# Layer 0 of a two-layer MLP in blocks of 512 tokens, weights converted in place, and attention banks shared

## The chip, the cores and the metric

One core of a Trainium2 chip runs the kernel. The metric is device time in microseconds of one execution, the median of several. The engines are TensorE (PE in the profile, its weight loads PEld), VectorE (DVE), ScalarE (ACT), GpSimd (POOL) and SyncE (SP), whose queue issues all DMAs here.

## What is computed

Sliding-window attention, then two MLP layers, all in float32. The weights come as float64 bits and are turned into float32 on the chip.

```python
# q, k, v: (4, 8, 576, 64); window 128; ALiBi slope per head
scores = where(0 <= i - j < 128, q @ k.T / 8 - slope * (i - j), -1e9)
x = softmax(scores) @ v            # -> (2304 tokens, 512)
h = maximum(x @ w_in, 0)           # layer 0, w_in (512, 2048)
x = (h * h) @ w_out                #          w_out (2048, 512)
h = x @ w2_in                      # layer 1
out = (h * cos(h)) @ w2_out
```

## The kernel before

**Tiling.** There are 18 blocks of 128 tokens for the attention; an attention step is one such block with two heads, so there are 72 steps. The 2048 hidden features of a layer are 16 `f` tiles of 128. A float32 operand of an MLP product is split into a high and a low part, and a product is three matmuls (hi·hi, lo·hi, hi·lo; lines 465 to 467 for `h`, 528 to 530 for `y`), each with weights of 128x128 and a moving operand of 256 or 512 tokens.

**Units.** The MLP work is a list of units, `ORDER`. In layer 0 a unit is 256 tokens and two `f` tiles, in layer 1 it is 512 tokens and one `f` tile; only layer 1's last block has 256 tokens. Each of these units writes one PSUM bank of `h` (2 x 256 or 512 float32) and adds to the banks of `y`. The first two and the last two blocks of layer 0 take turns (`CUTS`, `END_CUTS`): a block runs some `f` tiles, its partial `y` waits in SBUF (`YS`, `y_out`), and the other block follows.

**The main loop** (line 655) goes through the units. For unit i it emits: the softmax of an attention step, `h_mms(i + 1)`, the ReLU and square of unit i + 1 (`relu_part`, `square_part`), the transposes of the step, `y_mms(i)` and the step's product with V (`values`). `need` says how many attention steps must be out after each unit. Before the loop the first 16 steps run by themselves. A scheduler then sets the order on each engine, and each engine executes its list in that order.

**Weights.** `w_job` turns half an `f` tile (512 float64 per partition) into float32: a DMA into one of three `raw_w` buffers; `f64_top` (ACT) writes the upper half-words into `upper`, one tile for all; `f64_rest` (DVE) joins them with the lower bits into one of three `cv` buffers; `w_hi` (ACT) and `w_lo` (DVE) split that into `wh` and `wl`. Weights of layer 1 take the places of those of layer 0.

**PSUM** has eight banks: four for `y` and `h` of layer 0 (two each), two for the scores `s`, one for the transposes `t`, one for the attention output `o`. In the first 16 steps every other scores tile lies in an `h` bank (line 321).

Of the kernel before, what the change touches and what calls it, by code (L numbers as in the profile page):

```python
# [22 lines left out]
P = 128  # L23
NJ = NT // P
T = 256
# [19 lines left out]
ORDER = [  # L45
    (0, n, fs)
    for n0, n1, cuts in TURNS
    for a, b in zip(cuts, cuts[1:])
    for n in (n0, n1)
    if n is not None  # L50
    for fs in PAIRS[a:b]
]
ORDER += [(1, b, (f,)) for b in range(NB // 2) for f in range(NF)]
ORDER += [(1, NB // 2, fs) for fs in PAIRS]
NG1 = NB * NU
# [7 lines left out]
A_OPEN, W_OPEN, START_W, W1_FROM = 8, 1, 2, 64  # L63
# The first units leave more of their squares to the scalar engine.
ACT_UNITS = 20


class Job:
    """One piece of operand preparation: a load, then stages on ACT and DVE."""

    def __init__(self, key, load, stages, gates=None, source=None):
        self.key, self.load, self.stages = key, load, stages
        self.gates, self.source = gates or {}, source
        self.raw, self.at = None, 0
# [3 lines left out]
def attention_mlp_mlp(ctx: ExitStack, tc: tile.TileContext, kq, k0, q0, v, w1, w2, bias, ident, out):  # L78
    """Sliding-window ALiBi attention, relu^2 MLP, h*cos(h) MLP, in float32.

    Activations lie with features on the partitions and tokens on the free
    dimension.  A float32 operand of the MLP products is split exactly into
    hi + lo (float32r parts); a product is hi*hi + hi*lo + lo*hi.
    """
# [4 lines left out]
    cst = ctx.enter_context(tc.tile_pool(name="cst", bufs=1))  # L89
    wp = ctx.enter_context(tc.tile_pool(name="wp", bufs=1))  # L90
    rp = ctx.enter_context(tc.tile_pool(name="rp", bufs=4))
    cv = ctx.enter_context(tc.tile_pool(name="cv", bufs=3))
    xp = ctx.enter_context(tc.tile_pool(name="xp", bufs=1))
    gp = ctx.enter_context(tc.tile_pool(name="gp", bufs=2))
    yp = ctx.enter_context(tc.tile_pool(name="yp", bufs=2))
    dp = ctx.enter_context(tc.tile_pool(name="dp", bufs=1, space=DRAM))
    ps_y = ctx.enter_context(tc.tile_pool(name="ps_y", bufs=1, space=PSUM))
    ps_h = ctx.enter_context(tc.tile_pool(name="ps_h", bufs=2, space=PSUM))

    halfpi = cst.tile([P, 1], F32, name="halfpi")  # L100
    upper = cst.tile([P, 512], F32, name="upper")

    y1 = [dp.tile([P, KT * T], F32, name=f"y1_{n}") for n in range(NB)]

    WH, WL, A2, Y, YS = {}, {}, {}, {}, {}
# [7 lines left out]
    RAWS = {"a": 3, "w": 3}  # L113
# [19 lines left out]
    def advance(job):  # L133
        job.stages[job.at](job)
        if job.at == 1:
# [46 lines left out]
    def f64_rest(job):  # L182
        """The 19 lower bits of the significand, from the next 32 bits of the float64."""
        job.t = cv.tile([P, 512], F32, tag="cv", name="cv_" + "_".join(map(str, job.key)))
# [4 lines left out]
            upper.bitcast(I32),  # L189
# [14 lines left out]
    def w_job(layer, f, half):  # L204
        """Weights of layer 1 take their places when layer 0 has done with them."""
# [4 lines left out]
            [  # L210
                f64_top,
# [3 lines left out]
            {0: lambda: layer == 0 or now["y"] >= W1_FROM, 2: lambda: now["y"] >= max(last, default=-1)},  # L215
        )

    # x of two blocks of 256 tokens, hi and lo; layer 1 has a second such pair of tiles
    XS = [[xp.tile([P, 2, KT, T], F32R, name=f"x{part}_0") for part in "hl"]]

    def x_view(layer, n, part):
        pair = XS[0] if layer == 0 else XS[(n // 2 + 1) % 2]
        return pair[part][:, n % 2]

    def x_ready(layer, n):
        """Whether the units that read what x takes the place of have been emitted."""
        if layer == 0:
            old = [(0, n - 2)]
        else:
            old = [(1, n // 2 - 2)] if n >= 4 else [(0, NB - 1), (0, NB - 2)] if n >= 2 else []  # L230
        return now["h"] >= max((i for i, unit in enumerate(ORDER) if unit[:2] in old), default=-1)

    def x2_job(n, half):
        ks = slice(2 * half, 2 * half + 2)

        def hi(job):
            act.copy(x_view(1, n, 0)[:, ks], job.raw.rearrange("p (a t) -> p a t", a=2))

        def lo(job):
            r = job.raw.rearrange("p (a t) -> p a t", a=2)  # L240
            dve.tensor_tensor(x_view(1, n, 1)[:, ks], r, x_view(1, n, 0)[:, ks].bitcast(F32), ALU.subtract)

        return Job(
            ("x", n, half),
            lambda raw: sp.dma_start(raw, y1[n][:, half * 512 : half * 512 + 512]),
            [hi, lo],
            {0: lambda: len(XS) > 1 and x_ready(1, n)},
            ("y", n),
        )
# [63 lines left out]
    def scores(a):  # L313
        """Scores of one block of queries and two heads, and their exponentials."""
# [447 lines left out]
```

## Time and profile before

| | |
|---|---|
| time, median of 3 runs (lowest to highest) | 954.16 us (953.32 to 954.29) |
| profiled execution: span from first to last instruction | 950.9 us |
| median less that span | 3.3 us |
| PE busy / ACT busy / DVE busy | 932.8 / 528.0 / 604.9 us |

The profile gives one execution, and for it the span alone; what lies around the span is taken as 3.3 us. A matmul's busy time in the profile runs past the start of the next one, so what a matmul costs in a row of matmuls is read from the distance between starts, not from its busy time.

### The profile page before, as it was taken

What the parts mean: (1) busy time and instruction counts of PE and PEld (TensorE: products, weight loads), DVE (VectorE), ACT (ScalarE), POOL (GpSimd) and SP (SyncE); (2) the same over time, 40 slices, a digit from 0 to 9 for tenths busy, and PEclk for the clock granted to TensorE, in tenths of its full rate; (3) what the DMA queues carried; (4) which work ended last, traced back from release to release, by engine and by line L of the source; (5) the groups of instructions that cost most, each with busy time, mean ns of one, the idle gap of its engine ahead of it and who ended that gap; (6) DMA issues with size and microseconds to landing.
All of it is one profiled execution on the core that took longest, in us unless ns stands there. A gap on an engine that the chain in (4) does not pass through costs nothing.

```text
span 950.9 us, 16566 instructions
## 1 busy us (share of the span) xinstructions
PE 932.8 (98%) x6528; PEld 851.7 (90%) x6528; DVE 604.9 (64%) x1409; ACT 528.0 (56%) x1144; POOL 10.0 (1%) x37
## 2 busy tenths in 40 slices
PE   6899999999999999999999999999999999999998
PEld 6699989999999999999999988888888888888898
DVE  5998756555565666556648698566557566655564
ACT  5998766544444555445547586454445445444443
POOL 2000000000000000000000000000000000000000
PEclk9999999999999999999999999999999999999999
DMA  8576632112111121111117561011001100100010
GB/s 240 181 243 227 217 115 90 57 45 77 46 57 46 55 68 38 64 56 46 45 46 239 184 199 44 1 44 45 1 1 39 39 1 1 45 1 1 1 45 23
DMA packets 33965, 71.63 MB, mean 75 GB/s; under 512 B 3424, under 2 KB 10976, under 8 KB 33888
## 3 DMA queue, kind: packets, MB, share of 16 engines
q1 hardware_dynamic: 33888, 70.58, 23.0%
q8 instruction: 51, 0.84, 0.4%
q14 instruction: 26, 0.21, 0.1%
HBM read 61.13 MB, written 9.44 MB: 74 GB/s over the span
## 4 chain that ended last, share of the span: by engine, by line
PE 85%; DMA 5%; ACT 4%; DVE 4%; issue 1%; SPq 1%; ACTq 0%; DVEq 0%
PE y L528 13%; PE y L530 13%; PE y L529 13%; PE h L467 13%; PE h L466 12%; PE h L465 12%; DMA raw_w<-w_in 3%; PE o L423 3%; PE s L339 3%; PE t L406 3%; ACT upper L180 2%; DMA raw_a<-kq_in 1%; DVE cv_w L185 1%; ACT wh L198 1%; ACT p L381 1%
## 5 line engine op out<-in xcount | busy, mean ns | idle before, releaser
L467 PE MATMUL h<-xh,wl 128*128 128x256 f32 (+1 forms) x896 | 281.5, 314 | 0.0
L465 PE MATMUL h<-xh,wh 128*128 128x256 f32 (+1 forms) x896 | 280.7, 314 | 0.3 <-ACT wh L198 0.3
L466 PE MATMUL h<-xl,wh 128*128 128x256 f32 (+1 forms) x896 | 280.6, 313 | 0.0
L467 PEld LDWEIGHTS h<-xh,wl 128*128 128x128 f32 x896 | 170.9, 191 | 11.2 <-issue 1.2
L465 PEld LDWEIGHTS h<-xh,wh 128*128 128x128 f32 x896 | 170.7, 191 | 10.5 <-ACT wh L198 0.5
L466 PEld LDWEIGHTS h<-xl,wh 128*128 128x128 f32 x896 | 170.8, 191 | 9.9
L528 PE MATMUL y<-rh,wh 128*128 128x256 f32 x576 | 169.9, 295 | 1.4 <-ACT rh L479 0.9
L529 PE MATMUL y<-rl,wh 128*128 128x256 f32 x576 | 163.2, 283 | 1.8 <-DVE rl L483 1.8
L530 PE MATMUL y<-rh,wl 128*128 128x256 f32 x576 | 162.8, 283 | 0.0
L528 PE MATMUL y<-gh,wh 128*128 128x512 f32 (+1 forms) x320 | 117.8, 368 | 0.0
L529 PE MATMUL y<-gl,wh 128*128 128x512 f32 (+1 forms) x320 | 117.7, 368 | 0.0
L530 PE MATMUL y<-gh,wl 128*128 128x512 f32 (+1 forms) x320 | 117.7, 368 | 0.0
L528 PEld LDWEIGHTS y<-rh,wh 128*128 128x128 f32 x576 | 109.7, 191 | 7.4 <-issue 4.8
L529 PEld LDWEIGHTS y<-rl,wh 128*128 128x128 f32 x576 | 110.1, 191 | 2.9 <-DVE rl L483 2.6
L530 PEld LDWEIGHTS y<-rh,wl 128*128 128x128 f32 x576 | 110.0, 191 | 0.3 <-issue 0.3
L494 ACT ACTIVATE r<-r 128x512 f32<-128x512 f32 x72 | 45.5, 632 | 114.7 <-DVE r L493 114.6
L371 DVE CUSTOM_DVE_ANT_0 s<-s,bias_sb 128x256 f32<-128x256 f32 (+4 forms) x160 | 62.3, 392 | 55.3 <-PE s L339 37.5
L507 DVE TENSOR_TENSOR gl<-g,gh 128x512 fp32r<-128x512 f32 x72 | 49.8, 691 | 73.1 <-ACT gh L506 73.0
L381 ACT ACTIVATE p<-s,st 128x256 f32<-128x256 f32 (+4 forms) x160 | 70.5, 442 | 44.4 <-DVE st L371 42.2
L491 DVE SCALAR_TENSOR_TENSOR r<-kk,h 128x512 f32<-128x512 int32 x72 | 49.4, 686 | 63.5 <-ACT kk L490 63.5
L490 ACT ACTIVATE kk<-h 128x512 int32<-128x512 f32 x72 | 43.0, 597 | 69.8 <-PE h L467 69.6
L528 PEld LDWEIGHTS y<-gh,wh 128*128 128x128 f32 x320 | 60.3, 189 | 10.0
(63 smaller groups left out, 1312.8 us busy)
## 6 DMA issues: line engine op xcount, KB each, us to landing
raw_w<-w_in SPq DMA_DIRECT2D x64, 511.8 KB, 4.7
raw_a<-kq_in SPq DMA_DIRECT2D x56, 256.0 KB, 2.9
v<-v_in SPq DMA_DIRECT2D x18, 256.0 KB, 2.9
y<-ysb SPq DMA_DIRECT2D x18, 256.0 KB, 2.5
raw_a<-y SPq DMA_DIRECT2D x18, 256.0 KB, 2.8
out<-ysb SPq DMA_DIRECT2D x16, 256.0 KB, 2.9
k<-k_in SPq DMA_DIRECT2D x4, 256.0 KB, 5.5
q<-q_in SPq DMA_DIRECT2D x8, 128.0 KB, 5.5
```

What stands on the lines that cost most here:

```text
L371: dve.tensor_tensor_reduce(out=sbank[p0:p1, e, c0:c1], in0=sbank[p0:p1, e, c0:c1], in1=bias_sb[p0:p1, h, b0 + c0 : b0 + c1], scale=-0.125, ...
L381: act.activation(pt[p0:p1, e, c0:c1], sbank[p0:p1, e, c0:c1], AF.Exp, bias=st[p0:p1, e : e + 1], scale=-1.0, accum_out=st[p0:p1, 2 + e : 3 ...
L465: te.matmul(o, wh[:, cs], xh, start=(c == 0 and kt == 0), stop=False, skip_group_check=True)
L466: te.matmul(o, wh[:, cs], xl, start=False, stop=False, skip_group_check=True)
L467: te.matmul(o, wl[:, cs], xh, start=False, stop=(kt == KT - 1), skip_group_check=True)
L490: act.activation(kk, hb, AF.Copy, scale=INV2PI)
L491: dve.scalar_tensor_tensor(r, kk, -C1, hb, ALU.mult, ALU.add)
L494: act.activation(r, r, AF.Abs)
L507: dve.tensor_tensor(rl, g, rh.bitcast(F32), ALU.subtract)
L528: te.matmul(o, wh, gh, start=(first and m % per == 0), stop=False, skip_group_check=True)
L529: te.matmul(o, wh, gl, start=False, stop=False, skip_group_check=True)
L530: te.matmul(o, wl, gh, start=False, stop=last, skip_group_check=True)
```

## The change

Layer 0 goes over to units of 512 tokens and one `f` tile, like layer 1. Its order is: blocks 0, 1 and 2 of 512 tokens, one after the other; then block 3 (512 tokens) and block 4 (256 tokens) in turns, two units of block 3 and one of block 4 (with two `f` tiles) at a time. There are 72 units in layer 0 as before. All of a block's `f` tiles add up in its own `y` banks, so the partial sums in SBUF are gone. A list `MARKS` says how many attention steps are out by which unit.

A weight's `cv` buffer (two, not three) is set to zero by GpSimd, then `f64_top` writes into it and `f64_rest` joins in place; `upper` is gone. While the attention runs there are four `y` banks, one `h` bank, two banks that scores and transposes share, and one for `o`; the scores of the first 16 steps lie in the `y` banks. A finished `y` bank is copied into the buffers of the ReLU results (`a`, two of them) while the attention runs, and into those and two more afterwards. The cosine part of layer 1 works in place. The first 10 units, not 20, leave their squares to ACT.

```diff
-CUTS = (0, 1, 3, 5, 8)
-END_CUTS = (0, 4, 8)
-PAIRS = [(2 * u, 2 * u + 1) for u in range(NU)]
-TURNS = [(0, 1, CUTS)] + [(n, None, (0, NU)) for n in range(2, NB - 2)] + [(NB - 2, NB - 1, END_CUTS)]
+NBK = NB // 2
+ORDER = [(0, b, (f,)) for b in range(NBK - 1) for f in range(NF)]
+JOINT = len(ORDER)
+for u in range(NU):
+    ORDER += [(0, NBK - 1, (2 * u,)), (0, NBK - 1, (2 * u + 1,)), (0, NBK, (2 * u, 2 * u + 1))]
...
-ACT_UNITS = 20
+ACT_UNITS = 10
...
+    def f64_zero(job):
+        job.t = cv.tile([P, 512], F32, tag="cv", name="cv_" + "_".join(map(str, job.key)))
+        pool.memset(job.t, 0.0)
+
     def f64_top(job):
-        top = upper.bitcast(F16).rearrange("p (n two) -> p n two", two=2)
+        top = job.t.bitcast(F16).rearrange("p (n two) -> p n two", two=2)
...
-        if a < START and a % 2:
-            sbank = ps_h.tile([P, 2, 256], F32, tag="h", name=f"s_{a}")
+        if a < START:
+            sbank = ps_y.tile([P, 2, 256], F32, tag=f"y{a % 4}", name=f"s_{a}")
...
-        tb = ps_t.tile([P, 2, 2, P], F32, tag="t", name=f"t_{s}")
+        tb = ps_s.tile([P, 2, 2, P], F32, tag="s", name=f"t_{s}")
...
+    def h_slot(i):
+        if i >= NG1:
+            return ((ps_h, "h"), (ps_h2, "h"), (ps_y2, "z0"), (ps_y2, "z1"))[(i - NG1) % 4]
+        return (ps_h2 if ps_h2 is not None and i % 2 else ps_h), "h"
...
-        # partial sums of a block wait in SBUF for the rest of its f range
-        if (layer, n) in YS:
-            ysb = YS.pop((layer, n))
-            for b in range(2):
-                dve.tensor_tensor(ysb[:, b], Y[0][b], ysb[:, b], ALU.add)
...
+    def y_out(layer, b):
+        for k, yb in enumerate(Y.pop(b)):
+            if gp2 is not None and k % 2:
+                ysb = gp2.tile([P, 2, T], F32, tag="ysb", name=f"ysb_{layer}_{b}_{k}")
+            else:
+                ysb = gp.tile([P, 2, T], F32, tag="a", name=f"ysb_{layer}_{b}_{k}")
+            (dve.tensor_copy if k % 2 else act.copy)(ysb, yb)
+            if layer == 0:
+                sp.dma_start(y1[b][k], ysb.rearrange("p a t -> p (a t)"))
...
+    MARKS = [(-1, START), (14, 32), (29, 50), (30, 52), (45, 66), (48, STEPS)]
```

**What moves on TensorE, where the MLP begins.** In a tile's name the last number is a running one: before, `h_658` is the first unit's `h` (256 tokens), `o_551` is the output of attention block 3 and `t_570` a transpose. This is TensorE's list before, in the midst of the first unit:

```order
L466 MATMUL h_658<-xl_96,wh_1_654 128x256
L423 MATMUL o_551<-p_459,v_278 64x128 x2
L423 MATMUL o_551<-p_459,v_392 64x128 x2
L467 MATMUL h_658<-xh_95,wl_1_655 128x256
L406 MATMUL t_570<-id_sb,p_459 128x128 x4
L465 MATMUL h_658<-xh_95,wh_1_654 128x256
```

And now, with the waits; `h_652` is the first unit's `h` (512 tokens), `o_554` the output of attention block 3, `s_674` the scores of the 18th step:

```order
L419 MATMUL o_554<-p_530,v_281 64x128 [waits Activation_49]
L419 MATMUL o_554<-p_530,v_281 64x128
L419 MATMUL o_554<-p_530,v_395 64x128 x2
L335 MATMUL s_674<-KS,qh_1_513 128x256 [waits PE_49]
L335 MATMUL s_674<-KS,qh_1_513 128x256
L335 MATMUL s_674<-KS,ql_1_514 128x256 x2
L463 MATMUL h_652<-xh_100,wh_0_272 128x512 [waits Activation_49]
L464 MATMUL h_652<-xl_101,wh_0_272 128x512 [waits DVE_49]
L465 MATMUL h_652<-xh_100,wl_0_273 128x512
```

The first unit no longer stands among the products of the first 16 steps but behind all of them; it reads x of all four attention blocks.

**What moves on ScalarE, where one block of layer 0 ends and the next begins.** Before, in the middle of the attention, `ysb_3` is the result of block 3 (256 tokens), `a_` a ReLU result and `rh_` the high part of its square:

```order
L471 ACTIVATE a_3605<-h_3580 128x512 [waits PE_49]
L408 COPY p_3481<-t_3607 128x512 [waits PE_49]
L481 ACTIVATE rh_3613<-a_3605 128x512 [waits Activation_49]
L554 COPY ysb_3_3655<-y_0_3008 128x512 [waits PE_49]
L282 CAST qh_2_3576<-raw_a_3359 128x256 [waits PE_49]
```

And now at the end of the first block of 512 tokens, where `ysb_0_0` and `ysb_0_2` are copies of `y` banks 0 and 2:

```order
L539 COPY ysb_0_0_2057<-y_0_747 128x512
L377 ACTIVATE p_2074,st_2075<-s_2069,st_2075 128x256 [waits DVE_49] x2
L404 COPY p_1997<-t_2103 128x512 [waits PE_49]
L539 COPY ysb_0_2_2063<-y_2_749 128x512 [waits DMAHW1_49,Activation_49]
L277 CAST KS<-raw_a_2009 128x256 [waits DMAHW2_49]
L278 CAST qh_1_2011<-raw_a_1904 128x256 [waits PE_49]
L469 ACTIVATE a_2101<-h_2088 128x512 [waits DMAHW4_49,Activation_49]
```

The second copy and the next ReLU (`a_2101`) now wait for DMAs, those that empty their buffers.

**What is new on GpSimd.** Before, its list holds no weight at all. Now it holds 64 zeroings, here those of `f` tiles 5 and 6, between the zeroings of softmax tiles `p_`:

```order
L168 MEMSET cv_w_5_1_1055 128x512 [waits DVE_49,Activation_49]
L362 MEMSET p_862 64x2x64 [waits PE_49,Pool_49]
L363 MEMSET p_862 64x2x128
L360 MEMSET p_947 128x2x64 [waits PE_49,Activation_49,Pool_49]
L168 MEMSET cv_w_6_0_1100 128x512 [waits DVE_49]
```

A zeroing waits for DVE's last read of the buffer (`w_lo` of the half tile two before), and those of tile 6 stand behind softmax tiles that wait for TensorE.

## Rows read from the trace of the kernel before

**Rows 1.** The page, parts 1 and 2: busy time; TensorE's granted clock.

```profile
PE 932.8 (98%) x6528; PEld 851.7 (90%) x6528; DVE 604.9 (64%) x1409; ACT 528.0 (56%) x1144; POOL 10.0 (1%) x37
...
PEclk9999999999999999999999999999999999999999
```

**Rows 2.** The page, part 4: the chain that ended last, by engine.

```profile
PE 85%; DMA 5%; ACT 4%; DVE 4%; issue 1%; SPq 1%; ACTq 0%; DVEq 0%
```

**Rows 3.** Groups of TensorE's instructions by line and shape.

```profile
L465 PE MATMUL h<-xh,wh 128*128 128x256 f32 x640 | 181.1, 283 | 0.3 <-ACT wh L198 0.3
L528 PE MATMUL y<-rh,wh 128*128 128x256 f32 x576 | 169.9, 295 | 1.4 <-ACT rh L479 0.9 <-ACT ysb L554 0.5
...
L465 PE MATMUL h<-xh,wh 128*128 128x512 f32 x256 | 99.6, 389 | 0.0
```

**Rows 4.** Timeline of TensorE, layer 0 in its middle: start us, us, what.

```profile
300.33 0.28 PE L465 MATMUL h<-xh,wh 128*128 128x256 f32 x1
...
303.21 0.60 PE L406 MATMUL t<-id_sb,p 128*128 128x128 f32 x4
...
314.88 0.28 PE L465 MATMUL h<-xh,wh 128*128 128x256 f32 x1
```

**Rows 5.** The same in layer 1, units of 512 tokens.

```profile
651.13 0.39 PE L528 MATMUL y<-gh,wh 128*128 128x512 f32 x1
...
656.57 0.39 PE L528 MATMUL y<-gh,wh 128*128 128x512 f32 x1
```

**Rows 6.** TensorE by windows: window, us, busy (x instructions), clock, DMA share, GB/s.

```profile
0.00:50.00 50.00, 39.66 (x325) 1.00 0.70 210
50.00:200.00 150.00, 145.92 (x1229) 1.00 0.46 149
200.00:450.00 250.00, 250.00 (x2191) 1.00 0.18 56
```

**Rows 7.** The same windows, instructions on tile h alone.

```profile
0.00:50.00 50.00, 3.87 (x24) 1.00 0.70 210
50.00:200.00 150.00, 65.93 (x504) 1.00 0.46 149
200.00:450.00 250.00, 106.53 (x840) 1.00 0.18 56
```

**Rows 8.** The same windows, instructions on tile y alone.

```profile
0.00:50.00 50.00, 1.33 (x9) 1.00 0.70 210
50.00:200.00 150.00, 68.18 (x498) 1.00 0.46 149
200.00:450.00 250.00, 111.25 (x823) 1.00 0.18 56
```

**Rows 9.** Timeline of TensorE, its first matmul of the MLP.

```profile
37.24 0.36 PE L465 MATMUL h<-xh,wh 128*128 128x256 f32 x1
```

**Rows 10.** Timeline of ScalarE, x of the fourth attention block.

```profile
49.66 0.59 ACT L437 CAST xh<-o 128x512 fp32r<-128x512 f32 x1
```

**Rows 11.** All engines by windows: PE, PEld, DVE, ACT, POOL busy, then as rows 6.

```profile
50.00:100.00 50.00, 48.09 (x390) 46.88 (x389) 42.11 (x84) 43.54 (x88) 0.00 (x0) 1.00 0.72 239
...
200.00:250.00 50.00, 50.00 (x441) 48.78 (x440) 29.22 (x87) 24.58 (x66) 0.00 (x0) 1.00 0.20 65
```

**Rows 12.** Window 50 to 100 us, instructions on tile h, then on tile y alone.

```profile
50.00:100.00 50.00, 26.52 (x204) 1.00 0.72 239
...
50.00:100.00 50.00, 24.99 (x186) 1.00 0.72 239
```

**Rows 13.** The page, part 6: DMA issues, KB each, us to landing.

```profile
y<-ysb SPq DMA_DIRECT2D x18, 256.0 KB, 2.5
```

**Rows 14.** Groups on GpSimd: busy us, mean ns.

```profile
L617 POOL MEMSET upper<- 128x512 f32 x1 | 0.5, 517 | 0.0
```

**Rows 15.** Waits: us in total, times, longest us.

```profile
ACT p L381 <- DVE st L371: 42.2, 60, 5.3
...
ACT upper L180 <- DMA raw_w<-w_in: 12.2, 10, 2.3
```

More of the change, by code (lines that the diff above doesn't have):

```diff
@@ L34, with __init__ @@
 C2 = 2.0 * math.pi - C1
-CUTS = (0, 1, 3, 5, 8)
-END_CUTS = (0, 4, 8)
-PAIRS = [(2 * u, 2 * u + 1) for u in range(NU)]
-TURNS = [(0, 1, CUTS)] + [(n, None, (0, NU)) for n in range(2, NB - 2)] + [(NB - 2, NB - 1, END_CUTS)]
[L45 to L55, printed above, removed]
+NBK = NB // 2
[3 more added lines that the diff above has]
+    ORDER += [(0, NBK - 1, (2 * u,)), (0, NBK - 1, (2 * u + 1,)), (0, NBK, (2 * u, 2 * u + 1))]
+NG1 = len(ORDER)
+ORDER += [(1, b, (f,)) for b in range(NBK) for f in range(NF)]
+ORDER += [(1, NBK, (2 * u, 2 * u + 1)) for u in range(NU)]
+INDEX = {unit: i for i, unit in enumerate(ORDER)}
 START, LOOK, PLAIN = 16, 2, 4
-A_OPEN, W_OPEN, START_W, W1_FROM = 8, 1, 2, 64
-ACT_UNITS = 20
+A_OPEN, W_OPEN, START_W, W1_FROM = 8, 1, 2, JOINT - 2
+ACT_UNITS = 10
 class Job:
-    def __init__(self, key, load, stages, gates=None, source=None):
-        self.key, self.load, self.stages = key, load, stages
+    def __init__(self, key, load, stages, gates=None, source=None, frees=1):
+        self.key, self.load, self.stages, self.frees = key, load, stages, frees
         self.gates, self.source = gates or {}, source
@@ L188, in f64_rest @@
             13,
-            upper.bitcast(I32),
+            job.t.bitcast(I32),
             ALU.logical_shift_right,
@@ L210, in w_job @@
             [
+                f64_zero,
                 f64_top,
@@ L214, in w_job, with x_slot, x_ready, x2_job @@
             ],
-            {0: lambda: layer == 0 or now["y"] >= W1_FROM, 2: lambda: now["y"] >= max(last, default=-1)},
-        )
[L219 to L230, printed above, removed]
+            {0: lambda: layer == 0 or now["y"] >= W1_FROM, 3: lambda: now["y"] >= max(last, default=-1)},
+            frees=2,
+        )
+    XS = [[xp.tile([P, 2, KT, T], F32R, name=f"x{part}_{i}") for part in "hl"] for i in range(2)]
+    def x_slot(layer, b):
+        return (0, 1, 0, 1, 0)[b] if layer == 0 else (2, 0, 1, 2, 0)[b]
+    def x_ready(layer, b):
+        users = [(0, a) for a in range(NBK + 1)] + [(1, a) for a in range(NBK + 1)]
+        old = [u for u in users[: users.index((layer, b))] if x_slot(*u) == x_slot(layer, b)]
         return now["h"] >= max((i for i, unit in enumerate(ORDER) if unit[:2] in old), default=-1)
-    def x2_job(n, half):
-        ks = slice(2 * half, 2 * half + 2)
+    def x2_job(b, m):
+        def view(part):
+            x = XS[x_slot(1, b)][part]
+            return x[:, :, m, :] if b < NBK else x[:, 0, 2 * m : 2 * m + 2, :]
         def hi(job):
-            act.copy(x_view(1, n, 0)[:, ks], job.raw.rearrange("p (a t) -> p a t", a=2))
+            act.copy(view(0), job.raw.rearrange("p (a t) -> p a t", a=2))
         def lo(job):
             r = job.raw.rearrange("p (a t) -> p a t", a=2)
-            dve.tensor_tensor(x_view(1, n, 1)[:, ks], r, x_view(1, n, 0)[:, ks].bitcast(F32), ALU.subtract)
+            dve.tensor_tensor(view(1), r, view(0).bitcast(F32), ALU.subtract)
         return Job(
-            ("x", n, half),
-            lambda raw: sp.dma_start(raw, y1[n][:, half * 512 : half * 512 + 512]),
+            ("x", b, m),
+            lambda raw: sp.dma_start(raw, y1[b][m]),
             [hi, lo],
-            {0: lambda: len(XS) > 1 and x_ready(1, n)},
-            ("y", n),
+            {0: lambda: len(XS) > 2 and x_ready(1, b)},
+            ("y", b),
         )
@@ L441, in attention_mlp_mlp @@
     Hb, Aa, R2 = {}, {}, {}
-    ypools = [ps_y]
-    hpools = [ps_h]
+    ps_h2 = None
+    def h_slot(i):
+        if i >= NG1:
+            return ((ps_h, "h"), (ps_h2, "h"), (ps_y2, "z0"), (ps_y2, "z1"))[(i - NG1) % 4]
+        return (ps_h2 if ps_h2 is not None and i % 2 else ps_h), "h"
     def h_mms(i):
-        layer, n, fs = ORDER[i]
+        layer, b, fs = ORDER[i]
         if layer == 1:
-            run_until(("x", min(2 * n + 1, NB - 1), 1))
+            for m in range(KT if b < NBK else 2):
+                run_until(("x", b, m))
         for f in fs:
@@ L451, in h_mms @@
         now["h"] = i
-        hb = hpools[i % len(hpools)].tile([P, 2, T], F32, tag="h", name=f"h_{i}")
+        hpool, tag = h_slot(i)
+        hb = hpool.tile([P, 2, T], F32, tag=tag, name=f"h_{i}")
         Hb[i] = hb
@@ L520, in y_mms @@
             cols = slice(512 + m * P, 512 + m * P + P)
-            o = Y[0][m // per]
+            o = Y[b][m // per]
             if per == 2:
@@ new lines, in y_mms @@
+                y_out(layer, b)
+    def y_out(layer, b):
[7 more added lines that the diff above has]
+                sp.dma_start(y1[b][k], ysb.rearrange("p a t -> p (a t)"))
+            else:
+                dst = out[2 * b : 2 * b + 2][:, :, k * T : k * T + T]
+                sp.dma_start(dst.rearrange("n p t -> p n t"), ysb)
+        if layer == 0:
+            finished.add(("y", b))
@@ L572, in y_tail @@
             else:
-                act.copy(ysb[:, m], src)
-            sp.dma_start(out[NB - 1][:, m * T : m * T + T], ysb[:, m])
-    LA = 1
-    need = [0] * (NG1 + 1)
-    for i in range(NG1 - 1, -2, -1):
-        ahead = i + LA + 1
-        req = 8 * (ORDER[ahead][1] + 1) if 0 <= ahead < NG1 else 0
-        rate = 1 if 2 * NU <= i + 1 < NG1 - 2 * NU else 2
-        need[i] = min(STEPS, max(req, (need[i + 1] if i + 1 < NG1 else 0) - rate))
-    start_steps = max(need[-1], START)
-    need = [max(x, start_steps) for x in need]
+                act.copy(ysb, src)
@@ L588, in attention_mlp_mlp, with need @@
+            sp.dma_start(out[NB - 1][:, m * T : m * T + T], ysb)
+    MARKS = [(-1, START), (14, 32), (29, 50), (30, 52), (45, 66), (48, STEPS)]
+    def need(i):
+        for (i0, s0), (i1, s1) in zip(MARKS, MARKS[1:]):
+            if i <= i1:
+                return s0 + (s1 - s0) * (i - i0) // (i1 - i0)
+        return STEPS
+    start_steps = START
+    LA = 1
     pieces = [(f, half) for f in range(NF) for half in range(2)]
@@ L590, in attention_mlp_mlp @@
         queues["a"] += [kq_job(j, hp) for hp in range(4)]
-    queues["a"] += [x2_job(n, half) for n in range(NB) for half in range(2)]
+    queues["a"] += [x2_job(b, m) for b in range(NBK + 1) for m in range(KT if b < NBK else 2)]
     queues["w"] += [w_job(layer, *p) for layer in range(2) for p in pieces]
@@ L616, in attention_mlp_mlp @@
             pool.memset(Q0[j][0:64, :, 1, :], 0.0)
-        pool.memset(upper, 0.0)
         dve.memset(halfpi, math.pi / 2)
```

95 lines of the change are left out of this document (32 added, 63 removed).

## The prediction

> **What bounds the kernel now.** I read the page first: TensorE is busy for 932.8 of 950.9 us, at the full 2.4 GHz (a granted clock of nine tenths or more in every slice) [rows 1], and the chain that ended last lies on it for 85% [rows 2]. Such a busy share alone proves little here, since a matmul's busy time (283 ns with 256 tokens, 389 ns with 512 [rows 3]) overlaps that of the next. So I went on to the distances between starts. In layer 0 the 24 matmuls of `h` start at 300.33 and the next instruction at 303.21 us: 2.88 us, or 120.0 ns each [rows 4]. In layer 1 it is 24 matmuls in 651.13 to 656.57 us: 5.44 us, or 226.7 ns each [rows 5]. Neither stretch has a hole, so TensorE itself is the limit there, and a matmul's price is 120.0 ns for 256 tokens and 226.7 ns for 512. Doubling the tokens adds 106.7 ns, so 13.3 ns of either price come with the instruction and not with its tokens.
>
> The price of an attention step follows from the same stretch: from 300.33 to 314.88 us [rows 4] there are two units (96 matmuls, 11.52 us) and two steps, so a step takes (14.55 - 11.52) / 2 = 1.51 us of TensorE.
>
> With these prices the windows show where TensorE loses time. A step has 16 matmuls. From 200 to 450 us it starts 2191, of which 840 are for `h` and 823 for `y` [rows 6 to 8]: 1663 x 0.120 = 199.6 us, and 528 / 16 = 33 steps make 49.8 us; together 249.4 of 250 us. Nothing is lost. From 50 to 200 us it is 1002 x 0.120 = 120.2 us and 227 / 16 = 14.2 steps, 21.4 us: 141.7 of 150, so 8.3 us are lost. There the first weights are made: between 50 and 100 us ACT is busy for 43.54 and DVE for 42.11 of 50 us [rows 11]. The first 50 us are the attention's start; only 24 + 9 matmuls of the MLP lie in them [rows 7, 8].
>
> **The larger blocks.** Layer 0 has 9 blocks x 16 `f` tiles x 24 = 3456 matmuls of 256 tokens (`y` shows 576 on each of three lines [rows 3]). Now 4 blocks of 512 tokens take 4 x 16 x 24 = 1536 matmuls of 512, and 384 of 256 stay. So 3072 matmuls become 1536, and each pair saves 2 x 120.0 - 226.7 = 13.3 ns: 1536 x 13.3 = **20.5 us less**. This holds only while TensorE is the limit, as it is from 200 us on. Rounding of the starts (0.01 us over 24 matmuls) moves the price by less than 1 ns, the term by 1 us.
>
> The Trainium skill ("TensorE: Matmul & The Clock Gate", section Back-to-back issue gap) gives N / 2.4 + 2.5 ns for a warm matmul, so 109.2 and 215.8 ns: a pair would save 2.5 ns, and the whole term would be 3.8 us. The rows of this case show 120.0 and 226.7 ns with a weight load for every matmul, and the measurement decides.
>
> **The first unit starts later.** Before, its matmuls fill holes of the attention's start, from 37.24 us on [rows 9]. Now they stand behind all 16 steps and wait for x of the fourth attention block, whose cast begins at 49.66 us and takes 0.59 [rows 10]. The 33 matmuls that lay before 50 us [rows 7, 8] thus move behind it, 33 x 0.120 = 4.0 us, with about 1 us for the cast and the scores of a later step that also lay there: **5 us more**. ACT, which paces this stretch, loses the first unit's ReLU and square there and gains weights of later tiles instead; I count these as equal. Bounds: 3 us (the start gets as much shorter as ACT has less) and 6.
>
> **The first block with attention beside it.** While weights are made, units of block 0 now run with one step each; before, nearly no step ran until its end. The TensorE time of these steps is only moved. ACT's load is what counts: from 50 to 100 us it is 43.54 us for 204 + 186 = 390 matmuls of the MLP [rows 11, 12], 390 / 48 = 8.1 units, so 5.36 a unit; from 200 to 250 us it is 24.58 us for 441 matmuls [rows 11], 441 / 64 = 6.9 units with a step each, 3.6 for both; I put ReLU and square, two instructions of about 0.6, at 1.2, which leaves 2.4 for a step. So a unit with weights and step needs about 7.8 us of ACT, against 24 x 0.2267 + 1.51 = 6.95 us of TensorE. The busy times on ACT overlap too, so 7.8 is an upper bound, and I take it that TensorE stays just ahead. Weights are needed more slowly than before (one tile in 6.95 us, not 5.76), so ACT's waits for their DMAs (12.2 us in all [rows 15]) shrink, and the four evictions in turns with their sums fall away. I take **2 us less** of the 8.3; bounds: all 8.3 less, and 16 x (7.8 - 6.95) = 13.6 us more, if ACT sets the pace.
>
> Zeroing is 64 x 0.517 us [rows 14] on an engine that is busy for 10.0 us now [rows 1]; in steady state it lies between the last read of a buffer and the next half tile. With two `cv` buffers it can be late only in this block; its cost is in the bounds above.
>
> **Three hand-overs between blocks.** At the end of blocks 0, 1 and 2 the four copies of `y` go through two buffers, so the third waits for the landing of the first (2.5 us [rows 13]), and the next ReLU for that of the third. The chain is two copies (0.59 each by the cast of that size [rows 10]) and two landings, 6.2 us; beside it TensorE has the next unit's `h`, two steps' work and a `y`, some 7 us. It is late by little, and behind the waiting ReLU on ACT stand only the next square and exponentials. I take 1 us each, **3 us more**; bounds 0 and 3 x 6.2 = 19, where nothing hides it.
>
> **At nothing.** From the second block on a unit has about 1.2 steps, so 7.3 us of TensorE against 1.2 + 1.2 x 2.4 = 4.1 us of ACT. Scores and transposes in two banks: the next scores come one unit later, after the exponentials; uncovered it would be a wait for them on TensorE in each step. Turns at the end: layer 1's weights get 24 units, as long as the first weights had and without attention. Layer 1 keeps its units and its four `h` banks, so its 5.44 us a unit stay.
>
> **The sum.** -20.5 + 5 - 2 + 3 = -14.5 us. Against the profiled execution that is a span of 950.9 - 14.5 = 936.4; the median of the runs lies 3.3 us above the span, so the time is 939.7 us.
>
> **The rivals.**
> *The start and the hand-overs cost nothing much, and the first block's waits go.* -20.5 + 3 - 6 + 0 = -23.5: 930.7 us. For it: half of the 8.3 us may belong to the turns. Against: the new order puts the first unit behind the last step.
> *ACT sets the pace of the first block.* Then the third term is +13.6: -20.5 + 5 + 13.6 + 3 = 1.1, 955.3 us, and half of it gives 948. For it: 43.54 of 50 us before, and steps come on top; ACT executes its list in order, and one exponential alone waited up to 5.3 us for DVE [rows 15]. Against: ACT's true load is less than its busy sum.
> *One `h` bank is too few.* While the attention runs, `h` of unit i + 1 cannot start before the ReLU of unit i has read the bank; between them TensorE has only `y` of unit i - 1 and a step, 2.72 + 1.51 = 4.2 us. Whenever ACT comes to the ReLU later than that, TensorE stands. Averaged over 48 units, 0.3 us each eats the 14.5; at 0.5 us it is 24 us, 964 us. For it: long waits in ACT's list, as above. Against: outside the first block ACT is free for over 40% of the time (4.1 of 7.3 us).
> *The larger instruction saves nothing here.* If a matmul of 512 tokens in layer 0 took as long as two of 256, say because the attention between them spoils it, the sum would be 0 + 5 - 2 + 3 = +6: 960.2 us. Against it: [rows 4, 5], and layer 1 runs the same code.
> By the formula of the Trainium skill quoted above it would be nearly so, -3.8 + 5 - 2 + 3 = +2.2, 956.4 us.
>
> **Chances.** Forecast (933 to 946 us) 0.58; start and hand-overs nearly free (below 933) 0.14; ACT paces the first block (946 to 956) 0.16; one `h` bank (above 956) 0.09; no saving per matmul 0.03. The range 931 to 951 leaves out the lower third of the second case, the upper quarter of the third and the last two, about 0.2 in all. A measurement can tell about 0.2% from no change, 2 us: slower by more than that is the fourth case and 0.02 of the others, 0.11; within it 0.04; faster 0.85.
>
> **What the profile would show.** Right: some 222 matmuls in 50 us wherever the attention is over in layer 0, fewer TensorE starts overall (4992, not 6528), the first `h` just after 50 us, and waits of ACT on `a` for DMAs at three places. Wrong: `h` matmuls waiting for the ReLU's ACT through the whole attention, ACT full from 50 to 160 us with TensorE waiting for `wh` or `p`, or starts more than 230 ns apart in blocks of 512.

## The result and the profile after

The changed kernel takes 945.27 us (median of 4 runs, 943.62 to 948.23) against 954.22 in the same comparison: ratio 0.9903, 95% interval 0.9881 to 0.9925. Five rounds more (e9 below) gave 0.9905 (0.9887 to 0.9923). The gain is 9 us by the medians, where I forecast 14.5. The profiled execution lasted 944.3 us, 6.6 less than the one before; the one before was among the shorter of its kernel (the runs of that kernel beside e1 have spans of 951.0 to 955.2 us), so the two profiles show less of a gain than the medians.

The page of the changed kernel, against [rows 1, 2]: 4992 starts on TensorE, as forecast, and a larger share of the chain on it.

```profile
PE 921.9 (98%) x4992; PEld 768.4 (81%) x4992; DVE 599.4 (63%) x1403; ACT 522.9 (55%) x1134; POOL 43.3 (5%) x100
...
PE 88%; ACT 4%; DVE 4%; DMA 3%; issue 1%; SPq 0%; POOL 0%; ACTq 0%; DVEq 0%
```

TensorE's list in the changed kernel, in the middle of the attention. The first two rows and the last are the starts of `h` of units that lie two apart:

```profile
303.48 0.39 PE L463 MATMUL h<-xh,wh 128*128 128x512 f32 x1
303.71 0.39 PE L464 MATMUL h<-xl,wh 128*128 128x512 f32 x1
...
317.50 0.40 PE L463 MATMUL h<-xh,wh 128*128 128x512 f32 x1
```

These two units with two attention steps take 14.02 us; in [rows 4] the same work took 14.55. So the larger instruction saves here, but 0.53 us and not the 0.64 that 48 pairs at 13.3 ns give.

TensorE's list where the attention's start ends and the first unit begins:

```profile
40.64 0.95 PE L402 MATMUL t<-id_sb,p 128*128 128x128 f32 x4 [0.24 <-DVE p L393]
43.99 0.66 PE L419 MATMUL o<-p,v 128*64 128x128 f32 x8 [2.40 <-DVE xl L434]
...
53.94 0.49 PE L463 MATMUL h<-xh,wh 128*128 128x512 f32 x1 [0.36 <-ACT xh L433]
54.78 0.73 PE L464 MATMUL h<-xl,wh 128*128 128x512 f32 x1 [0.34 <-DVE xl L434]
55.31 0.63 PE L465 MATMUL h<-xh,wl 128*128 128x512 f32 x1
55.74 0.63 PE L463 MATMUL h<-xh,wh 128*128 128x512 f32 x1
56.16 0.63 PE L464 MATMUL h<-xl,wh 128*128 128x512 f32 x1
...
58.98 0.60 PE L402 MATMUL t<-id_sb,p 128*128 128x128 f32 x4
```

And TensorE's windows there; the columns are the length of the stretch, busy time and starts, granted clock, DMA share, GB/s:

```profile
40.00:45.00 5.00, 2.26 (x23) 0.96 0.45 152
45.00:50.00 5.00, 3.60 (x26) 0.70 0.18 63
50.00:55.00 5.00, 3.22 (x24) 0.99 0.61 204
55.00:60.00 5.00, 4.75 (x16) 0.67 0.65 232
```

The reader is to see three things: the first `h` starts at 53.94 us; before it TensorE stands for 2.40 us until x of attention block 2 has been read out of the one `o` bank; and behind it, and again as the first unit begins, the granted clock is below full, 0.70 and 0.67 as means of the two stretches, so it was at 1.2 and not 2.4 GHz for a part of them. At the lower level the `h` matmuls start 0.42 to 0.43 us apart, and the unit's 12 take 53.94 to 58.98 us, 5.04 instead of 2.72. The Trainium skill ("TensorE: Matmul & The Clock Gate", section Back-to-back issue gap) gives N / 1.2 ns for a matmul at the lower clock, 426.7 ns for 512 columns; the trace agrees.

**Where the time went.** Starts on `h`, `y` and `t` in the changed kernel, in this order, up to 75 us and from there to 200 (columns as above):

```profile
0.00:75.00 75.00, 12.26 (x43) 0.95 0.61 191
75.00:200.00 125.00, 48.23 (x199) 1.00 0.46 152
0.00:75.00 75.00, 5.90 (x24) 0.95 0.61 191
75.00:200.00 125.00, 51.99 (x204) 1.00 0.46 152
0.00:75.00 75.00, 12.55 (x64) 0.95 0.61 191
75.00:200.00 125.00, 10.93 (x72) 1.00 0.46 152
```

In the kernel before, the same windows had 127 and 403 starts of `h`, 96 and 408 of `y` (all of 256 tokens) and 56 and 60 of `t`. (An instruction at the border of a window is counted on both sides, and a step is counted by its four transposes, so what follows holds to about 1 us.) By 75 us the changed kernel is 223 - 2 x 67 = 89 matmuls of 256 behind, 44.5 x 0.2267 = 10.1 us, and two steps (8 of `t`) ahead, 3.1 us: 7.0 us behind, although its larger matmuls save 223 / 2 x 13.3 ns = 1.5 on this work. So the start cost 8.5 us. By 200 us it is 1034 - 2 x 470 = 94 matmuls behind, 10.7 us, and five steps ahead, 7.9 us; with the 6.9 us that the blocks had saved by then, 9.7 us are lost, 1.2 of them between 75 and 200 us. The rest of the layer must then have lost 20.5 - 9.7 - 6.6 = 4.2 us.

### The profile page after: what moved, and what is told of

Its sections match the earlier page's. It is cut to its first block, busy times and chain, and to the rows that moved or that the text cites. A ratio compares the mean times of both kernels' runs of the same rounds, so it can differ in the third digit from the quotient of the medians.

```text
span 944.3 us, 13513 instructions
## 1 busy us (share of the span) xinstructions
PE 921.9 (98%) x4992; PEld 768.4 (81%) x4992; DVE 599.4 (63%) x1403; ACT 522.9 (55%) x1134; POOL 43.3 (5%) x100
## 4 chain that ended last, share of the span: by engine, by line
PE 88%; ACT 4%; DVE 4%; DMA 3%; issue 1%; SPq 0%; POOL 0%; ACTq 0%; DVEq 0%
PE h L464 13%; PE h L463 13%; PE h L465 13%; PE y L524 13%; PE y L525 13%; PE y L526 13%; PE s L335 3%; PE o L419 3%; PE t L402 2%; DMA raw_a<-kq_in 2%; ACT p L377 1%; PE s L324 1%; DVE s L367 1%; ACT cv_w L175 1%; DVE cv_w L179 1%
## 5 line engine op out<-in xcount | busy, mean ns | idle before, releaser
L463 PE MATMUL h<-xh,wh 128*128 128x512 f32 (+1 forms) x640 | 237.3, 371 | 0.6 <-ACT xh L433 0.4
L464 PE MATMUL h<-xl,wh 128*128 128x512 f32 (+1 forms) x640 | 236.8, 370 | 0.3 <-DVE xl L434 0.3
L465 PE MATMUL h<-xh,wl 128*128 128x512 f32 (+1 forms) x640 | 236.3, 369 | 0.0
L465 PEld LDWEIGHTS h<-xh,wl 128*128 128x128 f32 x640 | 121.1, 189 | 20.3
L464 PEld LDWEIGHTS h<-xl,wh 128*128 128x128 f32 x640 | 121.1, 189 | 19.0 <-DVE xl L434 0.7
L524 PE MATMUL y<-rh,wh 128*128 128x512 f32 (+1 forms) x320 | 122.5, 383 | 0.8 <-DVE ysb L539 0.8
L525 PE MATMUL y<-rl,wh 128*128 128x512 f32 (+1 forms) x320 | 118.5, 370 | 0.0
L526 PE MATMUL y<-rh,wl 128*128 128x512 f32 (+1 forms) x320 | 118.4, 370 | 0.0
L503 DVE TENSOR_TENSOR gl<-r,gh 128x512 fp32r<-128x512 f32 x72 | 49.8, 691 | 75.1 <-ACT gh L502 75.0
L526 PEld LDWEIGHTS y<-rh,wl 128*128 128x128 f32 x320 | 60.3, 188 | 10.5
```

The costliest lines, as they stand in the source:

```text
L463: te.matmul(o, wh[:, cs], xh, start=(c == 0 and kt == 0), stop=False, skip_group_check=True)
L464: te.matmul(o, wh[:, cs], xl, start=False, stop=False, skip_group_check=True)
L465: te.matmul(o, wl[:, cs], xh, start=False, stop=(kt == KT - 1), skip_group_check=True)
L503: dve.tensor_tensor(rl, r, rh.bitcast(F32), ALU.subtract)
L524: te.matmul(o, wh, gh, start=(first and m % per == 0), stop=False, skip_group_check=True)
L525: te.matmul(o, wh, gl, start=False, stop=False, skip_group_check=True)
```

## The experiments

Each is compared with the kernel before; the changed kernel's ratio is 0.9903.

**e1: the size of the instruction alone**

```diff
-                te.matmul(o, wh[:, cs], xh, start=(c == 0 and kt == 0), stop=False, skip_group_check=True)
...
+                    halves = [(o[:, n], xh[:, n], xl[:, n]) for n in range(2)]
+                for n, (o_, xh_, xl_) in enumerate(halves):
...
+                    te.matmul(o_, wh[:, cs], xh_, start=first, stop=False, skip_group_check=True)
...
```

> The changed kernel with one edit: every matmul of layer 0 with 512 moving columns is issued as two of 256, so only the size of the instruction goes back; order, banks and copies stay. Theory A (the term of 20.5 us is real: 120.0 ns for 256, 226.7 ns for 512): 1536 pairs x 13.3 ns slower than the changed kernel's 945.3, so 965 to 966 us. Rival (the saving came from something else, such as the turns that went away): 945 to 950 us, because two instructions of 256 cost what one of 512 does; by the formula of the Trainium skill (TensorE: Matmul & The Clock Gate, section Back-to-back issue gap) it would be 3.8 us more, 949.

968.4 us (964.83 to 971.6), ratio 1.0146 (1.0124 to 1.0168): 23 us slower than the changed kernel by the medians, 20.1 by the profiled spans (964.4 and 944.3). Its trace, again two units with two steps:

```profile
329.69 0.28 PE L468 MATMUL h<-xh,wh 128*128 128x256 f32 x1
...
344.24 0.28 PE L468 MATMUL h<-xh,wh 128*128 128x256 f32 x1
```

14.55 us, as in [rows 4]. The larger instruction is where the gain comes from, and its size is near the 20.5 us of the forecast: the interval of the ratio leaves some 3 us either way around the 23, and this profiled execution was one of the shorter of its kernel. Everything else in the change, without the larger instruction, makes the kernel 1.5% slower than before.

**e2: a bank of their own for the transposes**

```diff
-        tb = ps_s.tile([P, 2, 2, P], F32, tag="s", name=f"t_{s}")
+        tpool, ttag = (ps_s, "s") if s < START else (ps_x, "t")
+        tb = tpool.tile([P, 2, 2, P], F32, tag=ttag, name=f"t_{s}")
...
+            if tag == "y" and layer == 0:
+                Y[b].append(Y[b][2])
```

> The changed kernel, but in layer 0 the products of y bank 3 are added into y bank 2 (this leaves the computation changed: two of the four y tiles are summed into one and stored twice), and the bank won that way holds the transposes alone, so scores have two banks of their own as before the change. Theory M (the 6 us more than forecast between 200 and 450 us come from scores and transposes sharing two banks): 4 to 6 us faster than the changed kernel's 945.3, 939 to 941. Rival S (sharing costs nothing, the missing microseconds are lost before 75 us): 945.3 within 1.5 us, the spread of its runs.

947.24 us (945.55 to 953.6), ratio 0.9934 (0.9911 to 0.9958): not faster. In its trace two units with two steps are as long as with shared banks (318.79 to 332.83, 14.04 us):

```profile
318.79 0.40 PE L465 MATMUL h<-xh,wh 128*128 128x512 f32 x1
...
332.83 0.40 PE L465 MATMUL h<-xh,wh 128*128 128x512 f32 x1
```

Sharing the banks costs nothing that can be told; theory M falls.

**e3: a second bank for `h`**

```diff
-        return (ps_h2 if ps_h2 is not None and i % 2 else ps_h), "h"
+        return ((ps_h2 or ps_x) if i % 2 else ps_h), "h"
```

> As the run before (y bank 3 summed into bank 2 in layer 0), but the bank won holds a second h, so h of a unit can begin before the ReLU of the unit ahead has read its bank. If one h bank is a limit (my third rival), TensorE's waits for the ReLU go and the time falls by 3 us or more, to 942 or less. Otherwise, since the trace of the changed kernel shows only 0.7 us of waits of the h weight loads for the ReLU, less than 1 us: 944 to 946.

944.83 us (943.25 to 946.56), ratio 0.9897 (0.9882 to 0.9913): no difference that can be told. A second `h` bank gains nothing here.

**e4: half of the hand-over left out**

```diff
+            if layer == 0 and b < NBK - 1:
+                if k < 2:
+                    ysb = gp.tile([P, 2, T], F32, tag="a", name=f"ysb_{layer}_{b}_{k}")
+                    (dve.tensor_copy if k % 2 else act.copy)(ysb, yb)
+                    for kk in (k, k + 2):
+                        sp.dma_start(y1[b][kk], ysb.rearrange("p a t -> p (a t)"))
+                continue
```

> The changed kernel, but at the ends of blocks 0, 1 and 2 only y banks 0 and 1 are copied out, each stored to two places (the copies of banks 2 and 3 are left out, and layer 1 reads wrong values), so no copy waits for the landing of another. If the three hand-overs cost what I put into the sum (1 us each), 942.3 us; at my upper bound of 6.2 us each, 927; if they cost as little as the one wait of 0.8 us of TensorE for a copy that the trace shows, 944.5 us.

945.17 us (944.27 to 946.19), ratio 0.9905 (0.9891 to 0.9918): the changed kernel's time, to within the 2 or 3 us that the two intervals leave. The one wait of TensorE at a hand-over that the changed kernel's trace shows is this row of its list; such a wait is absent from this run's waits, and the time is the same:

```profile
302.21 0.50 PE L524 MATMUL y<-rh,wh 128*128 128x512 f32 x1 [0.83 <-DVE ysb L539]
```

**e5: work that only fills the holes**

```diff
+            if 10 <= s < 16:
...
+                fill = ps_h.tile([P, 2, T], F32, tag="h", name=f"fill_{s}")
+                for n in range(12 if s == 12 else 4):
+                    te.matmul(fill[:, 0], WH[0, 0][:, 0:P], WH[0, 0][:, 0:T], start=n == 0, stop=True, skip_group_check=True)
             values(s)
```

> The changed kernel with 32 more matmuls of 256 columns among attention steps 10 to 15 of the start, on a first weight that is long there, into the empty h bank, read by nobody: they only keep TensorE at work in the holes between 30 and 53 us. In the changed kernel's trace TensorE has half its clock for two stretches of 3.4 us, near 45 and near 55 us, and in the second the h matmuls are 427 ns apart instead of 227. Theory C (these idle holes cost the clock, and the clock costs time): the clock is full throughout, and the time falls by 1.6 us for the second stretch, up to 3.4 for both: 942 to 943.7, although TensorE has 3.8 us more work. Rival L (only that the first unit begins late costs): the clock may be full, but the time stays at 945.3 or rises by up to 3.8 us.

944.85 us (942.04 to 949.38), ratio 0.9911 (0.9886 to 0.9935). The six runs fall apart by the mean granted clock of the execution: 942.04, 943.29 and 944.45 us at 0.998; 945.26 at 0.991, 949.38 at 0.989 and 947.94 at 0.987. The profiled one (942.04) had its clock back soon after 45 us, and its first `h` starts at 51.40 us:

```profile
40.00:45.00 5.00, 2.95 (x17) 0.68 0.48 157
45.00:50.00 5.00, 2.65 (x25) 0.98 0.65 221
50.00:55.00 5.00, 4.25 (x24) 1.00 0.41 147
55.00:60.00 5.00, 4.65 (x22) 1.00 0.63 209
```

In these six runs a lower clock goes with a longer time, as theory C has it. But filling these holes does not hold the clock up in every execution, and the median stays.

**e6: half of the first unit's `h` among the start's steps**

```diff
+    def h_half(n, kts):
...
+            te.matmul(o, wh, xh[:, n, kt], start=first, stop=False, skip_group_check=True)
...
+            if 11 <= s < 15:
+                h_half(0, (s - 11,))
             values(s)
```

> The changed kernel with the first unit's h cut in two: the 12 matmuls for its first 256 tokens (attention blocks 0 and 1) stand among attention steps 11 to 14 of the start, the 12 for the other 256 where all of them stood. Theory L (the late first unit costs, as in my sum): 12 x 226.7 ns behind the start become 12 x 120.0, 1.3 us less, and if the holes that are filled also keep the clock up, another 1.6: 942.4 to 944. Rival (the start is paced by ScalarE and VectorE and ends no sooner; the next wait takes the gain): 945.3 within 0.7 us.

941.96 us (941.18 to 943.35), ratio 0.9869 (0.9849 to 0.989): 3.3 us less by the medians; its interval and the changed kernel's overlap by a little, and so do the runs (943.35 at most here, 943.28 at least in the ten runs of the changed kernel). TensorE's list in its trace, where the other half of that `h` stands:

```profile
54.06 0.38 PE L453 MATMUL h<-xh,wh 128*128 128x256 f32 x1 [0.35 <-ACT xh L433]
54.90 0.38 PE L454 MATMUL h<-xl,wh 128*128 128x256 f32 x1 [0.46 <-DVE xl L434]
55.12 0.28 PE L455 MATMUL h<-xh,wl 128*128 128x256 f32 x1
55.24 0.28 PE L453 MATMUL h<-xh,wh 128*128 128x256 f32 x1
...
56.32 0.60 PE L402 MATMUL t<-id_sb,p 128*128 128x128 f32 x4
```

The start ends no sooner (54.06 against 53.94 us), as the rival had it, but behind it `h` takes 2.26 us, not 5.04: 1.28 us is less work, and the rest goes with the clock, which is full here (0.12 us apart). In these two profiles the unit ends 2.66 us sooner (56.32 against 58.98), and the span is 2.7 us shorter. Theory L holds; how much of the gain the clock has in other executions is not shown.

**e7: products and casts of x ahead of the next loads' casts**

```diff
-            tick("aw" if s < START_W else "a")
             values(s)
+            tick("aw" if s < START_W else "a")
```

> The changed kernel with two lines of the start in the other order: the product with V and the cast of x come before the casts of the next loads. In the changed kernel TensorE stands for 2.4 us at 41.6 us until x of attention block 2 is read out of the o bank, and on ScalarE that cast stands behind two casts of k and q, of which the second waits for its DMA until 41.92 us. If that order is what makes the hole, it shrinks, the first h comes before 53.9 us by 1 to 2.4 us, and the time is 943 to 944.5. Rival (the start ends when the last loads and casts do, whatever their order): 945.3 within 0.7 us.

946.41 us (943.63 to 948.07), ratio 0.9912 (0.9892 to 0.9931): nothing gained. The hole only changed what it waits for, and the first `h` starts at 54.21 us, no sooner:

```profile
42.30 0.66 PE L419 MATMUL o<-p,v 128*64 128x128 f32 x8 [1.98 <-ACT p L404]
```

**e8: the zeroing twice**

```diff
         pool.memset(job.t, 0.0)
+        pool.memset(job.t, 0.0)
```

> The changed kernel with every zeroing of a weight buffer on GpSimd done twice. My forecast puts the zeroing at nothing outside the first block and inside the bounds there: if it is off the path, 945.3 within 1 us. Rival (with two buffers the zeroing lies in the chain of the first block's weights, where ScalarE waits 12.4 us for GpSimd): 32 half tiles x up to 0.53 us, so 950 to 962.

946.73 us (945.61 to 948.43), ratio 0.992 (0.9902 to 0.9938). ScalarE's waits for the zeroing grew from the first row (the changed kernel) to the second (this run), by 9.8 us,

```profile
ACT cv_w L175 <- POOL cv_w L168: 12.4, 10, 1.6
```

```profile
ACT cv_w L176 <- POOL cv_w L169: 22.2, 29, 2.1
```

and the time by 1.5 us, less than these runs can tell from nothing; the two profiled executions have the same span, 944.3 us. So doing it a second time costs little or nothing here, and the first time no more.

**e9: the changed kernel again**

> The changed kernel itself once more, beside the next two, for the spread of its runs and the granted clock of each. Theory C (stretches at half clock in the start set the spread): the runs with the lower mean clock are the longer ones, by some 0.5 us for each 0.001 of the mean clock, as in the six runs with filling matmuls (0.998: 942.0, 943.3 and 944.5; 0.987 to 0.991: 945.3, 947.9 and 949.4). Rival: clock and time are not related.

946.01 us (943.28 to 946.81). Runs at a mean clock of 0.995 took 943.28, 944.23, 945.37 and 946.81 us, those at 0.990 and 0.987 took 946.66 and 946.77. The lower clock goes with the longer runs, but at 0.3 us or so for each 0.001, not 0.5, and runs at one clock differ by 3.5 us: here theory C explains only part of the spread.

**e10: e6 with fillers in what is left of the holes**

```diff
+                fill = ps_y.tile([P, 2, T], F32, tag="y0", name="fill")
+            if s >= 13:
+                for n in range(6):
+                    te.matmul(fill[:, 0], WH[0, 0][:, 0:P], WH[0, 0][:, 0:T], start=n == 0, stop=True, skip_group_check=True)
             values(s)
```

> The run with the first unit's h cut in two (941.96), and besides 18 matmuls of 256 columns that nobody reads, between the transposes and the products with V of attention steps 13 to 15. Theory C (the holes that are left cost the clock): the half clock between 40 and 50 us goes, and the time falls by 0.5 to 1.5 us, to 940.5 to 941.5. Rival (what is left of the start is paced by ScalarE and VectorE, so the clock of TensorE there does not matter): 942 within 0.7 us, or up to 1 us more for the added work.

943.57 us (940.77 to 945.23), ratio 0.9885 (0.9865 to 0.9905): by the median not better than e6. The profile is that of the fastest run, 940.77 us. In it the clock is full between 40 and 50 us and fell to 0.67 from 50 to 55; the other half of the first `h` begins 2.6 us sooner than in e6, and the span is 2.6 us shorter (939.0 against 941.6):

```profile
51.45 0.38 PE L453 MATMUL h<-xh,wh 128*128 128x256 f32 x1 [0.21 <-ACT xh L433]
```

So in this execution the time did follow. But its first products ran at the full clock earlier, too (see the last section), and the other four runs, at mean clocks of 0.993 to 0.996, took 941.74 to 945.23 us. Neither theory C nor the rival is decided.

**e11: fewer turns between small and large products**

```diff
-                scores_to(s + 1)
                 normalise(s)
...
             if todo > 0:
+                scores_to(s + 1)
                 transposes(s)
```

> The run with the first unit's h cut in two (941.96), and besides the scores of the next attention step stand right ahead of the transposes of the step before, so TensorE turns from products of 512 columns to the step's small ones three times in two units, not five times. Two units with two steps take 14.04 us in the changed kernel, 10.88 for the 48 large matmuls and 3.16 for the steps, against 3.03 before the change. Theory G (a turn from small products back to 512 columns costs: the matmuls behind it start 230 to 236 ns apart for a while): the period falls to 13.95 to 14.0 us, and the time by 1 to 2.5 us, to 939.5 to 941. Rival (the price belongs to the step's products themselves, or scores that come later make the softmax late): 14.04 us, and 942 or more.

947.78 us (946.28 to 949.45), ratio 0.993 (0.9912 to 0.9947), some 6 us slower than e6. Two units with two steps take 14.01 us, not 13.95:

```profile
317.81 0.39 PE L478 MATMUL h<-xh,wh 128*128 128x512 f32 x1
...
331.82 0.39 PE L478 MATMUL h<-xh,wh 128*128 128x512 f32 x1
```

Theory G falls: the number of turns hardly matters. What was lost lies in the first block, where the later scores make the softmax late. From 55 to 200 us TensorE's transposes wait for VectorE's part of it as below (us in total, times, longest); e6 has no such wait there:

```profile
PE t L402 <- DVE p L393: 5.9, 5, 2.3
```

**e12: work ahead of the first data**

```diff
+        dve.memset(zero, 0.0)
+        warm = ps_h.tile([P, 2, T], F32, tag="h", name="warm")
+        for n in range(18):
+            te.matmul(warm[:, 0, 0:P], zero, zero, start=n == 0, stop=True, skip_group_check=True)
         scores_to(0)
```

> The run with the first unit's h cut in two (941.96), and besides 18 matmuls of 128 columns on a tile of zeros in the first 4.5 us, while TensorE waits for its first data; nobody reads them. In the profiles the first products of the scores are 213 ns apart instead of 112 until some 8 us in some runs and until 13 to 17 us in others, and in those that stay long at half clock the start is later by 1.5 us. Theory C (this first half clock is paid in full): with work ahead of the first data the products are 112 ns apart from 4.5 us on, and the time falls by 1 to 2 us, to 940 to 941, with a smaller spread. Rival (the loads and ScalarE's exponentials pace the first 20 us): 942 within 0.7 us.

944.07 us (943.2 to 945.03), ratio 0.988 (0.9863 to 0.9896). The experiment spoiled itself: the trace shows the 18 matmuls as 36 starts that last until 7.6 us, so the first scores come 3 us later than in e6, at 0.11 us apart.

```profile
1.08 6.68 PE L642 MATMUL warm<-zero 128*128 128x128 f32 x36 [1.08 <-DVE zero L639]
7.60 1.95 PE L324 MATMUL s<-k,q 128*128 128x128 f32 x16
```

What the first half clock costs in the end stays open.

## Why the prediction was right, and where its sizes were off

The direction and the main term were right, and 945.27 lies in the range; the likeliest value of 939.7 was 5.6 us too low, because three terms on the other side were mis-sized. That it was not further off is in part luck: the hand-overs were put 2 us too dear, and of the 3.3 us taken to lie around the span some 1.3 belong to the short execution that was profiled (the runs of the kernel before beside e1 lie 1.9 to 2.1 us above their spans).

- **The larger blocks, 20.5 us.** Right: e1 takes back 20.1 us of span. The formula of the Trainium skill ("TensorE: Matmul & The Clock Gate", section Back-to-back issue gap) would have given 3.8 us for the term, and the trace does not agree with it.
- **The first unit starts later, 5 us.** Mis-sized: 8.5 us by 75 us, beyond my upper bound of 6. The 4.0 us of moved matmuls were right. The "about 1 us" beside them was 3.7: the first `h` starts at 53.94 us, and the cast that I took for it ended at 50.25 [rows 10]. And its 12 matmuls took 2.3 us too long, 0.34 of it a wait for `xl`, the rest at the lower clock. That makes 10.0 us, of which 1.5 were made up by 75 us; where is not shown. I had taken the clock as full because it was in every slice [rows 1]; but the change took the matmuls out of the holes of the start. In the profiles of e5 and e6, where matmuls stand in these holes again, the second stretch of lower clock is gone. In e7's the first unit runs at the full clock as well, and yet its span is 945.6 us, so what the clock alone costs stays open. e6 puts half of one unit back and gains 3.3 us.
- **The first block with attention beside it, -2 us.** Mis-sized: +1.2 us, inside the bounds. I had TensorE just ahead of ScalarE. In fact TensorE stood for 4.0 us between 75 and 200 us, each time for a result of ScalarE (3.0 us of such and other waits before the change). These are its waits there (us in total, times, longest), and all engines from 75 to 150 us, where most of the first weights are made (columns as in [rows 11]):

```profile
PE s L335 <- ACT p L404: 1.7, 1, 1.7
PE o L419 <- ACT p L404: 1.6, 2, 0.8
PE s L335 <- ACT p L377: 0.7, 1, 0.7
```

```profile
75.00:150.00 75.00, 71.05 (x401) 57.15 (x400) 63.05 (x164) 64.34 (x148) 12.29 (x25) 1.00 0.62 204
```

ScalarE is busy for 86% of this stretch, 6.4 us for each of its 10 units and not the 7.8 that I worked out, so it does not set the pace all along, but it comes late at single places. (My reason for calling 7.8 an upper bound was wrong: the 43.54 us of [rows 11] count overlapping instructions once; their durations add up to 51.1.) Neither the zeroing (e8) nor the one `h` bank (e3) is behind it; about 1 us is the dearer attention step of the next point.

- **The attention step of 1.51 us, which I carried over unchanged.** Mis-sized: (14.02 - 10.88) / 2 = 1.57 us, and for 56 steps 3.4 us, spread over both stretches. The bank that scores and transposes share is not the reason (e2), nor the number of turns from small to large products (e11). The starts of large matmuls behind small ones are 0.23 to 0.24 us apart for a while, in the rows from 303.48 us on; why, these runs don't settle. I had named starts more than 230 ns apart as a sign of being wrong, and for a part of the matmuls it came. In e1 the step is back at its old price, so by these prices e1 should have taken back 20.5 - 3.4 = 17.1 us; the 3 us beyond that are not placed.
- **Three hand-overs, 3 us.** Too dear: the trace shows the 0.83 us of one wait. TensorE's work hides the rest of the two landings, and e4 gains nothing without them. ScalarE's wait for a store's landing ahead of a ReLU was seen once, 0.5 us, not at three places.
- **At nothing.** Right for the shared banks, the second `h` bank and the zeroing, to within the 2 or 3 us that the runs can tell (e2, e3, e8).
- **The sum.** -20.5 + 8.5 + 1.2 + 4.2 = -6.6 us of span; the 4.2 after 200 us are what the other terms leave. Of them the steps explain 34 x 0.06 = 2.0 and the hand-over 0.8; 1.4 us are not placed.

Of the rivals, too few `h` banks is out (e3), and the larger instruction does save (e1). ScalarE as the pace of the first block is out by its size: the term came to 1.2 us, not 13.6 or half of it; no run here took work off ScalarE while the weights are made. The 222 matmuls in 50 us that I named for layer 0 after the attention were a slip: a third of the units there still has 256 tokens, and from 450 to 500 us there are 290. The best version that ran is e6, 941.96 us.

## What to carry to other kernels

A larger moving operand pays by the difference between the two distances of starts, and that could be read ahead from the trace fairly well here: 20.5 us forecast, 20.1 by the spans of e1 and 23 by the medians. What it costs lies where the larger block needs its data earlier: a block of twice the size waits for twice the input, and the small work that filled the holes of the start goes with it. Splitting only the first unit, so that half of it can run as soon as its half of the input is there, gives part of that back.

## What was not expected of the hardware

In the start, the same six products of the scores took 1.42 us in the changed kernel's profile (15.78 to 17.20) and 0.77 in that of e10 (14.18 to 14.95), as if the first had run at 1.2 GHz until some 17 us and the second no longer:

```profile
15.78 1.49 PE L324 MATMUL s<-k,q 128*128 128x128 f32 x6
17.20 0.49 PE L419 MATMUL o<-p,v 128*64 128x128 f32 x4
```

```profile
14.18 0.83 PE L324 MATMUL s<-k,q 128*128 128x128 f32 x6
14.95 0.44 PE L419 MATMUL o<-p,v 128*64 128x128 f32 x4
```

The column of the granted clock shows 1.00 from 10 to 17.5 us in both. But the record of the clock in these traces begins only at 17.33 us in the changed kernel's and at 7.33 us in e10's, both times at full, and the column, like a run's mean clock, takes the time ahead of it as full. So here the distances between starts tell more than the column, and the mean clocks in e5 and e9 leave out this first stretch. In the kernel before the record begins at 8.45 us, and the same six products took 0.76 us:

```profile
14.64 0.83 PE L328 MATMUL s<-k,q 128*128 128x128 f32 x6
15.40 0.44 PE L423 MATMUL o<-p,v 128*64 128x128 f32 x4
```

The changed kernel's profile is thus 1.8 us behind the one before at 17.20 us already, in products whose order the change left as it was. That this makes up 1.8 of the 8.5 us of the start is not shown: in the profiles of e7 and e8 the early products stand about 1 us ahead of the changed kernel's, and the first `h` starts at 54.21 and 54.72 us, no sooner than its 53.94. And what clock an execution gets is not set by the kernel alone: six runs of one kernel (e5) had mean clocks from 0.987 to 0.998 and times 7 us apart, more than most edits here are worth.
